# The output product of an attention and MLP kernel: seven block products with fifteen additions in place of eight

## The chip, the cores and the metric

The kernel runs on one core of one Trainium2 chip. The metric is device time in microseconds (us), the median of several runs; the kernel before takes 428.7 us.

Engine names as the profile has them: PE is the matrix engine (TensorE), PEld its weight loads, DVE is VectorE, ACT is ScalarE, POOL is GpSimd, SP is SyncE. A name with q (POOLq, SPq) is that engine's part that issues transfers. Tile names in the views: `st` is a loaded q or k, `c` its cast, `T` its transpose, `pt` the sigmoids, `xT` the attention result as FFN1 reads it, `hT` a block of h, `S` a sum of h, `wT` a sum of weights, `osb` an output tile, `ps_D` a pair of PSUM banks. The ramp is the start, up to about 25 us, in which the first attention tiles are made.

## The reference, cut to what matters

```python
# q, k, v: [8 batches, 12 heads, 448 tokens, 64]; w_gate, w_val: [768, 1536]; w_out: [1536, 768]
scores = q @ k.T / sqrt(64) - log(448)
attn   = sigmoid(scores) @ v                      # [8, 12, 448, 64]
x      = attn.transpose(0, 2, 1, 3).reshape(3584, 768)
h      = silu(x @ w_gate) * (x @ w_val)           # [3584, 1536]   "FFN1"
out    = h @ w_out                                # [3584, 768]    "output product"
```

The change concerns the last line alone. Inputs and output are fp32; the kernel multiplies in fp16 and bf16.

## The kernel before

The eight batches are worked through in four pairs of two. A pair has 24 FFN1 steps (two batches, twelve blocks `f` of 128 hidden features each), then the output product for its 896 tokens, in seven blocks `m` of 128 tokens. Between these units the program places "visits": pieces of attention for batches that come later. Each visit may also cast a q and a k tile that were loaded (`ready`), send them through a transposing DMA, and load the next q, k and v (`fetch`).

```python
def ffn2(pb, m):                      # one 128-token block of the output product: 24 matmuls
    osb = osp.tile([128, DM], FP32, tag="osb", name="osb")        # pool osp has bufs=3
    ...
    for half in range(2):             # output columns 0..383 and 384..767, one PSUM bank each
        for f in range(NF):           # NF = 12
            h = hT[(pb, f)].rearrange("p b s -> p (b s)")         # 128 features x 896 tokens
            nc.tensor.matmul(out=D.t[:, half, :hw], lhsT=h[:, m * 128:(m + 1) * 128],
                             rhs=wo16[f // FW][:, f % FW, half * hw:(half + 1) * hw],
                             start=(f == 0), stop=(f == NF - 1))
    ...                               # two evictions on VectorE into osb, then
    for i in range(2):
        (nc.sync if last else nc.gpsimd).dma_start(out=dsts[i], in_=osb[i * 64:(i + 1) * 64, :])
...
def w_load(kind, i):                  # a quarter of a weight matrix, cast to fp16 on the way
    if kind == "o":
        nc.gpsimd.dma_start(out=wo16[i], in_=moe_w_out[cs, :].rearrange(...))
...
def fetch(n):                         # loads of tile n: all three issued by GpSimd
    load(n, 0, G); load(n, 1, G); load_v(n)
def ready(n):
    cast(n, 0, G); cast(n, 1, G)      # casts on GpSimd
    if n >= NPE:
        trans_dma(n, 0); trans_dma(n, 1)          # issued by SyncE
...
begin[(8, 0)] += [lambda: ready(9), lambda: fetch(11)]            # what a visit starts
...
for i, at in enumerate(((6, 4), (7, 0), (7, 4), (8, 0))):
    begin[at].append(lambda i=i: w_load("o", i))                  # the four quarters of w_out
```

In the traces of this case an engine's instructions and its issues of transfers stand in program order (GpSimd's order after the change, shown below: sums to 104.54, then two casts, then loads, the last `wo` at 108.47). So GpSimd's queue holds the loads of q, k, v and `w_out`, the casts and, for the first three pairs, the output issues, one behind the other.

Of the kernel before, what the change touches and what calls it, by code (L numbers as in the profile page):

```python
# [9 lines left out]
FP32 = mybir.dt.float32  # L10
FP16 = mybir.dt.float16
BF16 = mybir.dt.bfloat16
SIGM = mybir.ActivationFunctionType.Sigmoid
MULT = mybir.AluOpType.mult


@with_exitstack
def kernel(
# [10 lines left out]
    nc = tc.nc  # L29
    ctx.enter_context(tc.manual_schedule())  # L30

    B, H, S, D = q.shape
    DM = H * D
    DFF = moe_w_gate.shape[1]
    C = S // D
    NJ = H // 4
    NP = H // 2
    NF = DFF // 128
# [3 lines left out]
    HREC = 1.0 / HSC  # L42

    qkscale = 1.0 / math.sqrt(D)
    sbias = -math.log(S)

    psD = ctx.enter_context(tc.tile_pool(name="psD", bufs=1, space=bass.MemoryType.PSUM))
    one = ctx.enter_context(tc.tile_pool(name="one", bufs=1))
    stg = ctx.enter_context(tc.tile_pool(name="stg", bufs=9))
    c16 = ctx.enter_context(tc.tile_pool(name="c16", bufs=4))  # L50
    v16p = ctx.enter_context(tc.tile_pool(name="v16p", bufs=6))
    qkT = ctx.enter_context(tc.tile_pool(name="qkT", bufs=4))
    ptp = ctx.enter_context(tc.tile_pool(name="ptp", bufs=10))
    xtp = ctx.enter_context(tc.tile_pool(name="xtp", bufs=12))
    htp = ctx.enter_context(tc.tile_pool(name="htp", bufs=13))
    tmp = ctx.enter_context(tc.tile_pool(name="tmp", bufs=2))
    osp = ctx.enter_context(tc.tile_pool(name="osp", bufs=3))
# [11 lines left out]

    ring = [psD.tile([128, 2, 512], FP32, tag=f"D{i}", name=f"ps_D{i}") for i in range(4)]  # L70
    ring_order = [0, 1, 2, 3]
# [4 lines left out]
    class Banked:  # L76
# [18 lines left out]
        def write(self, ins, bank, uses=None):  # L95
            if bank is not None:
                self.has_mm[bank] = True
                tc.add_to_no_dep_group(self.mm[bank], ins.ins)
                p = self.prev
                if p is not None and p.has_rd[1 - bank] and (uses is None or p.made != uses):  # L100
                    tc.declare_no_dep(ins.ins, group=p.rd[1 - bank], reason="the other bank")
# [9 lines left out]
    FW = 3  # L111
# [3 lines left out]
    wo16 = [one.tile([128, FW, DM], FP16, tag=f"wo{i}", name=f"wo16_{i}") for i in range(NW)]  # L115
# [7 lines left out]
            nc.gpsimd.dma_start(out=dst, in_=w[:, cs].rearrange("(j p) n -> p j n", p=128))  # L123


    qkv_st = {}
    q16, v16, qT = {}, {}, {}

    def src_of(n, which):
        b, j = divmod(n, NJ)  # L130
        return (q, k, v)[which][b, 4 * j:4 * j + 4].rearrange("(h w) (p c) d -> (w p) h (c d)", w=2, c=C)

    def load(n, which, eng=None):
        st = stg.tile([128, 2, S], FP32, tag="stg", name=f"st{which}_{n}")
        (eng or nc.sync).dma_start(out=st, in_=src_of(n, which))  # L135
        qkv_st[(n, which)] = st

# [5 lines left out]
    def cast(n, which, eng, lo=0, hi=C):  # L143
        st = qkv_st[(n, which)]
        if hi == C:
            qkv_st.pop((n, which))
        t = c16.tile([128, hi - lo, 2, D], BF16, tag="c16" if hi - lo == C else f"c16_{lo}", name=f"c16_{which}_{n}")
        q16[(n, which, lo)] = t
        (eng.copy if eng is nc.scalar else eng.tensor_copy)(  # L149
            out=t.rearrange("p c h d -> p h c d"),  # L150
            in_=st.rearrange("p h (c d) -> p h c d", c=C)[:, :, lo:hi, :],
        )
# [96 lines left out]
    hT = {}  # L249
# [13 lines left out]
    def ffn1(b, f):  # L263
        D = Banked("f", made=(b // 2, f))
        for prs in (range(NP - 2), range(NP - 2, NP)) if f == 0 else (range(NP),):
            ffn1_mm(D, b, f, prs)
        ffn1_gate(D, b, f)

    def ffn1_gate(D, b, f):
        s16 = tmp.tile([128, S], FP16, tag="s16", name="s16")  # L270
        D.read(nc.scalar.activation(out=s16, in_=D.t[:, 0, :S], func=SIGM), 0)  # L271
        t1 = tmp.tile([128, S], FP16, tag="t1", name="t1")
        D.read(nc.vector.tensor_tensor(out=t1, in0=D.t[:, 0, :S], in1=s16, op=MULT), 0)  # L273
        if b % 2 == 0:
            hT[(b // 2, f)] = htp.tile([128, 2, S], FP16, tag="hT", name=f"hT_{b // 2}_{f}")
        D.read(
            nc.vector.scalar_tensor_tensor(  # L277
                out=hT[(b // 2, f)][:, b % 2, :], in0=D.t[:, 1, :S], scalar=HSC, in1=t1, op0=MULT, op1=MULT
            ),
            1,  # L280
        )

    def ffn2(pb, m):
        hw = DM // 2
        osb = osp.tile([128, DM], FP32, tag="osb", name="osb")
        dsts = []
        for i in range(2):
            bb, c = divmod(2 * m + i, C)
            bb += 2 * pb
            dsts.append(out[bb * S:(bb + 1) * S, :].rearrange("(p c) n -> c p n", c=C)[c])  # L290
        D = Banked("o")
        for half in range(2):
            for f in range(NF):
                h = hT[(pb, f)].rearrange("p b s -> p (b s)")
                D.write(
                    nc.tensor.matmul(  # L296
                        out=D.t[:, half, :hw],
                        lhsT=h[:, m * 128:(m + 1) * 128],
                        rhs=wo16[f // FW][:, f % FW, half * hw:(half + 1) * hw],
                        start=(f == 0),  # L300
                        stop=(f == NF - 1),
                    ),
                    half,
                    uses=(pb, f),
                )
        last = pb == B // 2 - 1
        end = last and m == C - 1
        for half in range(2):
            hs = slice(half * hw, (half + 1) * hw)
            if end and half == 1:  # L310

                for i in range(2):
                    r = slice(i * 64, i * 64 + 64)
                    oe = osp.tile([128, hw], FP32, tag=f"oe{i}", bufs=1, name=f"oe{i}")
                    if i == 0:
                        ev = nc.scalar.activation(
                            out=oe[r], in_=D.t[r, 1, :hw], func=mybir.ActivationFunctionType.Copy, scale=HREC
                        )
                    else:
                        ev = nc.vector.tensor_scalar(  # L320
                            out=oe[r], in0=D.t[r, 1, :hw], scalar1=HREC, scalar2=None, op0=MULT
                        )
                    D.read(ev, 1)
                    (nc.scalar if i == 0 else nc.sync).dma_start(out=dsts[i][:, hs], in_=oe[r])
            else:
                D.read(
                    nc.vector.tensor_scalar(  # L327
                        out=osb[:, hs], in0=D.t[:, half, :hw], scalar1=HREC, scalar2=None, op0=MULT
                    ),
                    half,  # L330
                )
                if end:
                    for i in range(2):
                        nc.sync.dma_start(out=dsts[i][:, hs], in_=osb[i * 64:(i + 1) * 64, hs])
        if not end:
            for i in range(2):
                (nc.sync if last else nc.gpsimd).dma_start(out=dsts[i], in_=osb[i * 64:(i + 1) * 64, :])  # L337


    FU1, FU2 = 2.26, 3.9  # L340
    units = []
    f1_start, f1_end = {}, {}
    tt = 0.0
    for pb in range(B // 2):
        for b in (2 * pb, 2 * pb + 1):
            f1_start[b] = tt
            for f in range(NF):
                if b or f > 2:
                    units.append((FU1, ffn1, (b, f)))
                tt += FU1  # L350
            f1_end[b] = tt
        for m in range(7):
            units.append((FU2, ffn2, (pb, m)))
            tt += FU2


    FIRST, PER = f1_end[0] - 5.0, 38.5
    tiles = [(n, c) for n in range(NJ, NQ) for c in range(C)]
    visits = [tiles[:2], tiles[2:4]]
    for i in range(0, len(tiles), C):  # L360
# [2 lines left out]
    for grp in visits:  # L363
        n, c = grp[0]
        b, j = divmod(n, NJ)
# [17 lines left out]

    V, G = nc.vector, nc.gpsimd
    load(0, 1, nc.scalar)
    for n, which in ((0, 0), (1, 0), (1, 1), (2, 0), (2, 1), (3, 0), (3, 1)):
        load(n, which)
# [8 lines left out]
    def fetch(n):  # L396
        load(n, 0, G)
        load(n, 1, G)
        load_v(n)

    def ready(n):
        cast(n, 0, G)
        cast(n, 1, G)
        if n >= NPE:
            trans_dma(n, 0)
            trans_dma(n, 1)
# [71 lines left out]
    begin = {(n, c): [] for n in range(NJ, NQ) for c in (0, 4)}  # L478
# [7 lines left out]
    begin[(7, 4)] += [lambda: fetch(10)]  # L486
    begin[(8, 0)] += [lambda: ready(9), lambda: fetch(11)]
    begin[(8, 4)] += [lambda: ready(10)]
    for i, at in enumerate(((6, 4), (7, 0), (7, 4), (8, 0))):
        begin[at].append(lambda i=i: w_load("o", i))  # L490
    for n in range(9, NQ):
# [9 lines left out]
    for dur, fn, args in units:  # L501
        if vi < len(visits) and tcur >= vtime[vi]:
            group = visits[vi]
# [49 lines left out]
```

## Time and profile before

| | before |
|---|---|
| time, median | 428.7 us (428.35 to 429.27, 4 runs) |
| profiled span | 426.6 us |
| PE busy | 415.9 us, 97% |
| output matmuls | 672, 163 ns apart |
| POOL busy | 117.5 us, 28% |
| landing of an output issue | 3.1 us median (GpSimd's queue) |

The views that the prediction reads are shown in it. This is the list of transfers in the stretch 100 to 140 us, around the output product of the first pair: output and source, issuing queue, count, size, median time from issue to landing.

```profile
out_dram<-osb POOLq DMA_DIRECT2D x14, 192.0 KB, 3.2
...
T<-c SPq DMA_TRANSPOSE x8, 5.9
```

Fourteen outputs, seven blocks, land in 3.2 us at the median (7.9 at the longest) although loads and transposes run in the same stretch. A block takes 3.9 us and uses one of three output tiles, and visits come between. So the tile whose output was issued at 108.97 is written again, by VectorE's next eviction into it, only at 120.97, 12 us later.

### The profile page before, as it was taken

What the parts mean: (1) busy time and instruction counts of PE and PEld (TensorE: products, weight loads), DVE (VectorE), ACT (ScalarE), POOL (GpSimd) and SP (SyncE); (2) the same over time, 40 slices, a digit from 0 to 9 for tenths busy, and PEclk for the clock granted to TensorE, in tenths of its full rate; (3) what the DMA queues carried; (4) which work ended last, traced back from release to release, by engine and by line L of the source; (5) the groups of instructions that cost most, each with busy time, mean ns of one, the idle gap of its engine ahead of it and who ended that gap; (6) DMA issues with size and microseconds to landing.
All of it is one profiled execution on the core that took longest, in us unless ns stands there. A gap on an engine that the chain in (4) does not pass through costs nothing.

```text
span 426.6 us, 7903 instructions
## 1 busy us (share of the span) xinstructions
PE 415.9 (97%) x3261; PEld 217.6 (51%) x3261; DVE 204.9 (48%) x337; ACT 211.9 (50%) x291; POOL 117.5 (28%) x167
## 2 busy tenths in 40 slices
PE   6899999999999999999999999999999999999995
PEld 2544544545555444545555544544555545555663
DVE  2726656555324555555323556555433356555322
ACT  4966885654624755656433755746433642222000
POOL 5564346401637346000345545000221100000000
PEclk8799999999999999999999999999999999999999
DMA  8999999995699997500298996600162300000234
GB/s 301 231 277 211 210 190 208 177 247 99 152 218 174 194 174 178 115 0 2 71 229 169 226 193 164 120 0 2 23 131 71 81 0 2 0 2 0 55 94 111
DMA packets 57796, 54.38 MB, mean 127 GB/s; under 512 B 35680, under 2 KB 52448, under 8 KB 57760
## 3 DMA queue, kind: packets, MB, share of 16 engines
q0 software_dynamic: 20896, 39.20, 40.9%
q1 hardware_dynamic: 36512, 14.13, 20.3%
q8 instruction: 25, 0.41, 0.4%
q10 hardware_dynamic: 352, 0.56, 0.4%
q14 instruction: 11, 0.09, 0.1%
HBM read 47.19 MB, written 11.01 MB: 136 GB/s over the span
## 4 chain that ended last, share of the span: by engine, by line
PE 91%; ACT 3%; DVE 2%; issue 1%; DMA 1%; ACTq 0%; DVEq 0%
PE ps_D L256 50%; PE ps_D L296 26%; PE ps_D L197 8%; PE ps_D L228 7%; ACT pt L215 2%; DMA st<-in_q_dram 1%; PE ps_D L171 1%; DVE t L273 1%; ACT s L271 1%; ACT pt L212 1%; DVE T L180 0%; DVE hT L277 0%; DVE xT L237 0%; DVE xT L245 0%; ACT xT L243 0%
## 5 line engine op out<-in xcount | busy, mean ns | idle before, releaser
L215 ACT ACTIVATE pt<-ps_D,sb_t 128x896 f16<-128x896 f32 x148 | 140.3, 1014 | 84.4 <-PE ps_D L197 84.2
L256 PE MATMUL ps_D<-xT,wg 128*128 128x448 f16 x576 | 126.9, 353 | 0.9 <-ACT pt L215 0.5
L256 PE MATMUL ps_D<-xT,wv 128*128 128x448 f16 x576 | 126.4, 352 | 0.0
L296 PE MATMUL ps_D<-wo,hT 128*128 128x384 f16 x672 | 111.8, 326 | 0.0
L273 DVE TENSOR_TENSOR t<-ps_D,s 128x448 f16<-128x448 f32 x96 | 59.9, 624 | 92.3 <-ACT s L271 92.0
L271 ACT ACTIVATE s<-ps_D 128x448 f16<-128x448 f32 x96 | 52.7, 549 | 90.6 <-PE ps_D L256 80.1
L296 PEld LDWEIGHTS <-hT 128*128 128x128 f16 x672 | 64.8, 98 | 46.4 <-issue 4.3
L256 PEld LDWEIGHTS <-wg 128*128 128x128 f16 x576 | 53.7, 98 | 58.5 <-issue 12.4
L256 PEld LDWEIGHTS <-wv 128*128 128x128 f16 x576 | 56.4, 98 | 52.8 <-issue 0.3
L327 DVE TENSOR_SCALAR osb<-ps_D 128x384 f32<-128x384 f32 x55 | 30.7, 558 | 74.2 <-PE ps_D L296 71.0
L277 DVE SCALAR_TENSOR_TENSOR hT<-ps_D,t 128x448 f16<-128x448 f32 x96 | 60.0, 625 | 10.4 <-DVE t L273 0.5
L337 POOL DMA_DIRECT2D out_dram<-osb x42 | 22.4, 537 | 146.1 <-DVE osb L327 146.1
L149 POOL CAST c<-st 128x896 bf16<-128x896 f32 (+1 forms) x42 | 38.8, 936 | 63.1 <-issue 29.6
L197 PE MATMUL ps_D<-T,T 64*64 64x448 bf16 x672 | 47.4, 367 | 2.3 <-ACT T L180 1.1
L228 PE MATMUL ps_D<-pt,v 64*64 64x448 f16 x672 | 36.2, 351 | 0.3 <-ACT pt L215 0.3
L197 PEld LDWEIGHTS <-T 64*64 64x64 bf16 x672 | 16.3, 107 | 25.9 <-issue 18.2
L237 DVE CAST xT<-ps_D 128x448 f16<-128x448 f32 x24 | 15.0, 625 | 29.8 <-PE ps_D L228 23.0
L245 DVE CAST xT<-ps_D 64x448 f16<-64x448 f32 x46 | 28.6, 622 | 0.7
L228 PEld LDWEIGHTS <-v 64*64 64x64 f16 x672 | 19.9, 108 | 13.0 <-issue 1.5
L212 ACT ACTIVATE pt<-ps_D,sb_t 128x448 f16<-128x448 f32 x40 | 23.0, 631 | 0.0
L140 POOL DMA_DIRECT2D v<-in_v_dram x24 | 17.7, 738 | 0.1
L135 POOL DMA_DIRECT2D st<-in_k_dram x20 | 14.7, 736 | 3.1 <-DMA wv<-in_moe_w_val_dram 3.1
(25 smaller groups left out, 59.6 us busy)
## 6 DMA issues: line engine op xcount, KB each, us to landing
st<-in_q_dram POOLq DMA_DIRECT2D x20, 448.0 KB, 4.8
st<-in_k_dram POOLq DMA_DIRECT2D x20, 448.0 KB, 7.0
out_dram<-osb POOLq DMA_DIRECT2D x42, 192.0 KB, 3.1
v<-in_v_dram POOLq DMA_DIRECT2D x24, 224.0 KB, 8.3
wg<-in_moe_w_gate_dram POOLq DMA_DIRECT2D x4, 576.0 KB, 14.4
wv<-in_moe_w_val_dram POOLq DMA_DIRECT2D x4, 576.0 KB, 14.6
wo<-in_moe_w_out_dram POOLq DMA_DIRECT2D x4, 576.0 KB, 14.7
out_dram<-osb SPq DMA_DIRECT2D x12, 192.0 KB, 2.7
```

The source lines that it names most:

```text
L149: (eng.copy if eng is nc.scalar else eng.tensor_copy)(out=t.rearrange("p c h d -> p h c d"), in_=st.rearrange("p h (c d) -> p h c d", c=C) ...
L197: nc.tensor.matmul(out=sc[w * 64:(w + 1) * 64, h2, :S], lhsT=kt[r, w * 64:(w + 1) * 64], rhs=qt[r, :, w * 64:(w + 1) * 64], start=True, st ...
L212: nc.scalar.activation(out=pt[:, h2, :], in_=sc[:, h2, :S], func=SIGM, bias=sb_t, scale=qkscale), h2
L215: nc.scalar.activation(out=pt, in_=sc[:, :, :S], func=SIGM, bias=sb_t, scale=qkscale)
L228: nc.tensor.matmul(out=P[g:g + 64, h2, :S], lhsT=vt[r, h2, c * D:(c + 1) * D], rhs=pt[r, h2, :], start=(c == 0), stop=(c == C - 1),)
L245: nc.vector.tensor_copy(out=o, in_=i)
L256: nc.tensor.matmul(out=D.t[:, i, :S], lhsT=w16[f // FW][:, pr, cs], rhs=xT[(b, pr)], start=(pr == 0), stop=(pr == NP - 1),),
L271: D.read(nc.scalar.activation(out=s16, in_=D.t[:, 0, :S], func=SIGM), 0)
L273: D.read(nc.vector.tensor_tensor(out=t1, in0=D.t[:, 0, :S], in1=s16, op=MULT), 0)
L277: nc.vector.scalar_tensor_tensor(out=hT[(b // 2, f)][:, b % 2, :], in0=D.t[:, 1, :S], scalar=HSC, in1=t1, op0=MULT, op1=MULT),
L296: nc.tensor.matmul(out=D.t[:, half, :hw], lhsT=h[:, m * 128:(m + 1) * 128], rhs=wo16[f // FW][:, f % FW, half * hw:(half + 1) * hw], start ...
L327: nc.vector.tensor_scalar(out=osb[:, hs], in0=D.t[:, half, :hw], scalar1=HREC, scalar2=None, op0=MULT),
```

## The change

The intent is to take matmuls off PE, which is the bound. For two token blocks `g` and `g + 3` of a pair, the 256 tokens by 1536 features of h and the 1536 by 768 of `w_out` are each cut into two by two parts. Eight part products (48 matmuls) become seven (42 matmuls), in Winograd's form of Strassen's algorithm with fifteen additions: four sums of h, four of the weights, seven of products. Part of the seven are made in PSUM, where a product is added onto another; the rest are made by VectorE as it evicts. The sums of h and of the weights go to GpSimd. One block of each pair stays direct, and so does group 0 of the first pair, which is 144 direct matmuls and 11 groups of 42 = 462.

```diff
+    def w_sums():                       # once: 8 instructions of 128 x 1152
+        for s in range(2):
+            ...
+            for kind in (3, 2, 1, 4):
+                ...
+                nc.gpsimd.tensor_tensor(out=t, in0=a, in1=b, op=op)
+    def h_sums(pb, f):                  # per pair: kind 3 for f < 6, the trio 1, 2, 4 for f >= 6
+            ...
+            nc.gpsimd.tensor_tensor(out=t, in0=a, in1=b, op=op)     # 128 x 384
     def ffn1(b, f):
         ...
         ffn1_gate(D, b, f)
+        if b % 2:
+            h_sums(b // 2, f)
+    def ffn2_group(pb, g):              # two blocks, seven products
+        o1 = osp.tile([128, DM], FP32, tag="osb", name="osb")
+        mm(1, 0, True, False)           # product number, PSUM bank, start, stop; 6 matmuls
+        snap(0, o1, 0)                  # evict a bank into a half of an output tile
+        mm(2, 1, True, True)
+        put(1, o1, 0)                   # evict and add onto what the tile holds
+        mm(6, 0, False, False)
+        snap(0, o1, 1)
+        mm(5, 1, True, False)
+        o2 = osp.tile([128, DM], FP32, tag="osb", name="osb")
+        snap(1, o2, 1)
+        mm(7, 0, False, False)
+        put(0, o2, 1)
+        mm(3, 1, False, True)
+        put(1, o1, 1)                   # o1 is complete only here
+        mm(4, 0, False, True)
+        eng = nc.sync
+        ...                             # o1 issued; then snap(0, o2, 0) and o2 issued
@@ schedule @@
-        for m in range(7):
-            units.append((FU2, ffn2, (pb, m)))
+        o_units = [(FU2, ffn2, (pb, C - 1))]
+        for g in range(3):
+            if pb == 0 and g == 0:
+                o_units += [(FU2, ffn2, (pb, m)) for m in (g, g + 3)]
+            else:
+                o_units.append((FU3, ffn2_group, (pb, g)))
-    FIRST, PER = f1_end[0] - 5.0, 38.5
+    FIRST, PER = f1_end[0] - 5.0, 37.3
+    begin[(9, 0)] += [w_sums]
```

Cut: the token and weight slices of the products, the direct blocks, which are now ordered so that the last features come last, smaller pools elsewhere to make room for the sums, and outputs moved from GpSimd's queue to SyncE's. Among the smaller pools are those of the loaded q and k tiles (9 to 4 tiles, the first six apart) and of the v tiles (6 to 5).

## The prediction

> **What bounds the kernel now.** I read the page's busy shares first, then the chain that ended last, then PE's own order of time. Busy shares and chain:
>
> ```profile
> PE 415.9 (97%) x3261; PEld 217.6 (51%) x3261; DVE 204.9 (48%) x337; ACT 211.9 (50%) x291; POOL 117.5 (28%) x167
> ...
> PE 91%; ACT 3%; DVE 2%; issue 1%; DMA 1%; ACTq 0%; DVEq 0%
> ```
>
> PE is busy 97% of the span and is 91% of the chain, so PE's order is the clock of the kernel. A busy PE is not always a PE at its rate, so I took single stretches from the time order of PE, around the end of the first FFN1 pair and in one output block:
>
> ```profile
> 97.83 1.31 PE L256 MATMUL ps_D<-xT,wg 128*128 128x448 f16 x6
> 98.98 1.30 PE L256 MATMUL ps_D<-xT,wv 128*128 128x448 f16 x6
> ...
> 129.72 4.07 PE L296 MATMUL ps_D<-wo,hT 128*128 128x384 f16 x24
> 133.63 0.54 PE L256 MATMUL ps_D<-xT,wg 128*128 128x448 f16 x2
> ```
>
> Columns are start, length, engine. 24 output matmuls take 133.63 - 129.72 = 3.91 us, 163 ns each, with no gap before or after. Removing output matmuls therefore pays in full, if nothing makes PE wait instead. PE has no slack after 22 us in which a new wait could be absorbed.
>
> The other thing to see is GpSimd's order of time, since the change puts work there. Here are the loads of q/k/v (`st`, `v`) and of the output weights `wo` before they are needed:
>
> ```profile
> 60.49 0.72 POOL L135 DMA_DIRECT2D st<-in_q_dram  x1
> 61.21 0.72 POOL L135 DMA_DIRECT2D st<-in_k_dram  x1
> 61.93 0.73 POOL L140 DMA_DIRECT2D v<-in_v_dram  x1
> 62.65 0.78 POOL L120 DMA_DIRECT2D wo<-in_moe_w_out_dram  x1
> ...
> 81.22 0.94 POOL L149 CAST c<-st 128x896 bf16<-128x896 f32 x1 [4.02 <-issue]
> 82.10 0.73 POOL L135 DMA_DIRECT2D st<-in_q_dram  x1
> 82.82 0.74 POOL L135 DMA_DIRECT2D st<-in_k_dram  x1
> 83.54 0.75 POOL L140 DMA_DIRECT2D v<-in_v_dram  x1
> 85.50 0.77 POOL L120 DMA_DIRECT2D wo<-in_moe_w_out_dram  x1 [1.21 <-DMA wo<-in_moe_w_out_dram]
> ```
>
> These issues run well ahead of PE: the first group belongs in the program to an attention visit that PE reaches only at 73.6 us. Even so, in the window 82 to 87 us the last `wo` needs 15.8 us to land, so it is there at 85.5 + 15.8 = 101.3 us. PE starts the output product at 100.1 us and reads the last quarter of `wo` at its tenth matmul, 100.1 + 9 x 0.163 = 101.6 us. The weights arrive **just in time**; the stretches from 60 to 100 us have the DMA share at 0.96 to 1.27, saturated.
>
> **What the Trainium skill says.** "TensorE: Matmul & The Clock Gate", section "Wait — 56ns, not 53.3ns?", gives N/2.4 GHz plus about 2.5 ns per warm matmul: 162.5 ns for N = 384. The trace has 163: it agrees. Its Part 1 says that an idle PE of some 3.4 us drops to half clock and needs about as long to recover; the trace before has no such idle time once started. "GPSIMD Engine Reference", section 3.1, has a two-input `tensor_tensor` at about 2.6 cycles an element, 4497 ns for 2048 fp32; the kernel before has no such instruction, only one-input casts (896 elements, 937 ns). "DMA: Bandwidth & Descriptors", section "SWDGE vs HWDGE vs iDMA", ties a cast during DMA to GpSimd's queue; so the `wo` and `v` loads, which cast to fp16, stay in GpSimd's order, as the trace has them. "SBUF — State Buffer", section "Who interferes with whom", says a VectorE instruction with at most one SBUF input and no 2-port mode does not contend with GpSimd. The gates and evictions here read PSUM plus at most one SBUF tile, and nearly all casts on GpSimd keep to 0.93 to 0.94 us, so I add no contention.
>
> **Part by part.**
>
> *Removed.* The order of the changed program on PE has 144 direct and 462 Strassen output matmuls, 606 for 672: eleven groups save 6 each. 66 x 0.163 = **-10.8 us** on PE, all on the path.
>
> *Added on VectorE.* Seven evictions a group for four: 33 more at 0.558 us (the row `osb<-ps_D`), 18 us on an engine that is 48% busy. Products take 6 x 0.163 = 0.98 us and alternate between two banks, so an eviction (0.56 us and some 0.2 to start) fits behind the other bank's product. Where the xT copies of an attention visit come just ahead (after 129.5 us they hold VectorE to 131.4, when a group begun at 129.7 would want its first eviction at 130.9), the third product waits about 0.4 us. Some four such places: **+1.5 us**.
>
> *Added on GpSimd.* 96 h sums of 384 columns and 8 weight sums of 1152. Estimate from the skill's 4497/2048 = 2.2 ns an element: 0.85 us, with start cost about 0.93 us for an h sum and 2.6 us for a weight sum. A trio that waits on itself is about 3.0 us. In all about 96 x 0.95 + 8 x 2.6 = 112 us, less 42 output issues moved to SyncE (22 us): GpSimd rises from 117 to about 207 us, still under half the span. By share it is harmless; by order it is not.
>
> *Moved: the order on GpSimd.* The first FFN1 pair's h sums stand in GpSimd's order **ahead of** the loads that the visits issue. The order of the changed program reads: sums of f = 0, 1, 2 of the second batch; loads of tile 8 and wo 0; sums 3, 4; casts 8; loads 9, wo 1; sums of 5, 6, 7; loads 10, wo 2; sums of 8, 9, 10; casts 9; loads 11, wo 3. Each sum waits for VectorE's gate of that f, so GpSimd can no longer run ahead of PE. I step through it with PE's times of before:
>
> - gate of f = 2 ends at 74.5 (its `hT` instruction 73.84 + 0.62): sum to 75.6; loads 8 and wo 0, 4 issues, to 78.6; sums 3, 4 to 80.9.
> - casts 8 wait for the k load: issued at 76.4 and landing after 7.2 us (that of 60 to 64 us in the trace before): 83.6, done at 84.8. Loads 9 and wo 1 to 87.8.
> - sum 5 to 88.7, trios 6 and 7 to 94.7; loads 10 and wo 2 to 97.7.
> - trios 8, 9, 10 to 106.7 (gate of 10 done at 96.6: GpSimd is late by its own work); casts 9 to 108.6; loads 11 to 110.8; **wo 3 issued at about 110.8**, not 85.5.
> - The four `wo` loads before landed after 10.1 (little ahead of it) to 19.6 us (two fetches ahead). With 10 to 14: about 121 to 125.
>
> PE needs wo 3 at 101.6 and wo 2 (issued 96.9, there about 108) at 101.1. So the first direct block waits some 20 to 23 us: **+21 us**. A bound that doesn't use my estimate for the sums: the gate of f = 10 at 96.6, three sums of at least 0.5 each, casts 1.8, issues 2.2, landing 10.1 gives 112.2: at least 10.6 us of wait.
>
> *Follow-ups.* An idle PE of this length comes back at half clock, by the skill: **+1.7 us**. The wait then hides the weight sums: they start about 116.5 after the last trio and casts 10 and end by 137.5; PE, resumed at 122.5, has 17 direct matmuls, 48 more, two visits, and two products of group 1 before it reads a weight sum, about 16 us, 138. Later pairs have all loads far ahead; trios of 3.0 us against FFN1 steps of 2.27 put GpSimd about 5 us behind at the end of a pair, which the direct block (3.9 us) and two products cover to within **+0.5 us**.
>
> Sum: 428.7 - 10.8 + 1.5 + 21 + 1.7 + 0.5 = 442.6. I choose 441, a little under, because the skill's rate is for fp32 and fp16 sums may be quicker.
>
> **Rivals.** (1) *The saving arrives whole*: 428.7 - 10.8 + 1 to 3 = 419 to 421. For it: every engine's share allows it, and later pairs show no obstacle. Against it: the lower bound of 10.6 us, which stands on program order and landing times alone. (2) *Quick sums*: at 0.6 us a sum, the same stepping issues wo 3 at 104.7 and lands it at 115: a wait of 13 us and 433. (3) *VectorE takes over*: 33 more evictions, of which two per product pair wait for each other through the banks. At 0.56 of 0.98 us per product I see no bound; if each group lost 0.5 us, 11 x 0.5 = 5.5 us, 446. (4) *The DMA hides it*: if the wo quarter landed in 5 us because queues are empty, 6 us less, 435; the emptiest landing seen is 10.1.
>
> **Range and chances.** 13 us of wait and no extras gives 431; 25 us with all extras 447, with some room for a contention I left out. Range 432 to 449. Within 2% ends at 437.3, that is a wait of about 16 us with the extras: quick sums or a quick landing, 0.14. Faster than 420.1 needs the order argument to be wrong: 0.04.
>
> **What would show it.** In the profile after: (a) PE output matmuls 606, the same 163 ns; (b) one idle stretch of PE near 101 to 122 us, in the first direct block, released by a `wo` DMA; (c) GpSimd's issue of the last `wo` near 110 us, behind h sums; (d) h sums of about 0.9 us, weight sums 2.6; (e) no wait of over 0.6 us within a group on VectorE; (f) later pairs shorter than before by about 2.9 us each. It is wrong if PE shows no idle stretch there (order on GpSimd not binding), if sums take 0.5 us or less, or if a second long wait appears at the weight sums or at the casts behind them.

## The result, and the profile after

The changed kernel is correct and takes **452.05 us** (450.65 to 453.58, 4 runs) against 428.7 us (428.35 to 429.27, 4 runs) of the kernel before in the same rounds. The ratio is 1.0544, 95% interval 1.0502 to 1.0586: slower by 5.4%. A ratio here and below is fast runs compared with fast runs of the same rounds, so it is not quite the ratio of the medians. The profiled run has a span of 451.8 us and a mean granted clock of 0.962. The direction was predicted; the time lies 11 us above the 441 predicted and 3 us above the range.

The busy shares and the chain that ended last, from the page after:

```profile
PE 412.8 (91%) x3195; PEld 212.9 (47%) x3195; DVE 222.7 (49%) x370; ACT 211.8 (47%) x291; POOL 199.7 (44%) x229
...
PE 74%; DMA 9%; POOL 5%; ACT 4%; DVE 4%; issue 2%; SPq 0%; DVEq 0%; ACTq 0%; POOLq 0%
PE ps_D L266 41%; PE ps_D L377 14%; PE ps_D L207 6%; PE ps_D L238 6%; PE ps_D L450 5%; DMA out_dram<-osb 4%; POOL S L340 3%; ACT pt L225 3%; DMA wo<-in_moe_w_out_dram 2%; DMA st<-in_k_dram 1%; POOL st L144 1%; PE ps_D L181 1%; DVE t L285 1%
```

PE has 66 instructions fewer, as intended, and is no longer the chain alone: 9% of the span is waiting for transfers, 5% is GpSimd. The transfer with the largest share is not `wo`, which the prediction spoke of, but an **output**. The time order of PE has both. First the direct blocks behind the first pair's FFN1 (start, length, engine and line, operation, count, then the idle time before it and what ended it):

```profile
101.00 0.98 PE L450 MATMUL ps_D<-wo,hT 128*128 128x384 f16 x5
106.49 0.96 PE L450 MATMUL ps_D<-wo,hT 128*128 128x384 f16 x3 [4.52 <-DMA wo<-in_moe_w_out_dram]
119.18 4.99 PE L450 MATMUL ps_D<-wo,hT 128*128 128x384 f16 x16 [11.72 <-DMA wo<-in_moe_w_out_dram]
124.10 0.76 PE L207 MATMUL ps_D<-T,T 64*64 64x448 bf16 x12
```

A block of 24 matmuls that took 3.9 us before now lasts from 101.00 to 124.10, 23.1 us: 16.24 us of wait for the last two quarters of `wo`, and the last 16 matmuls take 4.92 us, 0.31 each, at about half clock (granted clock 0.54). Here is GpSimd's order of time just ahead of that:

```profile
102.70 0.91 POOL L340 TENSOR_TENSOR S<-S,hT 128x384 f16<-128x384 f16 x1
103.68 0.91 POOL L340 TENSOR_TENSOR S<-hT,S 128x384 f16<-128x384 f16 x1
104.54 1.81 POOL L159 CAST c<-st 128x896 bf16<-128x896 f32 x2
106.29 0.75 POOL L144 DMA_DIRECT2D st<-in_q_dram  x1
107.03 0.73 POOL L144 DMA_DIRECT2D st<-in_k_dram  x1
107.75 0.74 POOL L149 DMA_DIRECT2D v<-in_v_dram  x1
108.47 0.79 POOL L124 DMA_DIRECT2D wo<-in_moe_w_out_dram  x1
```

GpSimd is never idle here; it is late by its own sums, and the last `wo` goes out at 108.47 instead of 85.50. It is there when PE resumes: 119.18 - 108.47 = 10.7 us to landing.

The second loss stands in one group of each of the first two pairs: group 2 of the first pair (from 142.98) and group 1 of the second, the second of its three (from 238.19). PE in the second pair's:

```profile
238.19 2.11 PE L377 MATMUL ps_D<-wo,hT 128*128 128x384 f16 x12
240.15 3.09 PE L377 MATMUL ps_D<-wT,S 128*128 128x384 f16 x18
249.34 2.08 PE L377 MATMUL ps_D<-wo,S 128*128 128x384 f16 x6 [6.11 <-DVE osb L388]
251.21 2.12 PE L377 MATMUL ps_D<-wT,hT 128*128 128x384 f16 x6
```

PE waits for VectorE's eviction at line 388. VectorE, however, is the messenger; its own order of time and the transfers issued in the stretch 237.5 to 240 us say what it waited for:

```profile
248.73 0.56 DVE L388 TENSOR_SCALAR osb<-ps_D 128x384 f32<-128x384 f32 x1 [6.85 <-DMA out_dram<-osb]
```

```profile
out_dram<-osb SPq DMA_DIRECT2D x4, 192.0 KB, 9.8
```

The eviction is the first one into `o2` of group 1. With three tiles and two per group, that is the tile that was `o1` of group 0, the group before; its output was issued from 238.01 on and took 9.8 us to land. In the third pair's groups (337 to 364 us), which also have three tiles and their sums on GpSimd, but no loads beside them, fourteen outputs take 2.9 us at the median and PE's longest wait is 0.24 us. What else was under way shows in GpSimd's order: the q, k and v loads of a visit were issued at 235.28, 236.02 and 236.74, late, behind three trios of sums, and took 4.8, 10.6 and 12.2 us to land; the two transposes issued from 234.49 on took 2.9 and 10.7 us. The table by stretch shows the DMA engines full (busy time of PE, PEld, DVE, ACT and POOL, granted clock, then the mean busy share of the DMA engines, which can exceed 1 in this profile, and GB/s); in the stretch 237 to 240 us before it the share was 0.99:

```profile
240.00:243.00 3.00, 3.00 (x20) 1.83 (x19) 1.12 (x2) 0.00 (x0) 0.93 (x1) 1.00 1.64 144
```

The account of the difference of the spans, 451.8 - 426.6 = 25.2 us, read from these views:

| part | us | how read |
|---|---|---|
| 66 matmuls fewer | -10.8 | 66 x 0.163 |
| direct block, `wo` late | +19.1 | 23.10 - 3.95 (two such blocks take 7.90 before); 16.2 wait, the rest half clock |
| group 2 of pair 1, output tile | +4.7 | 142.98 to 154.57 is 11.6, for 42 x 0.163 = 6.85 |
| group 1 of pair 2, output tile | +8.2 | 238.19 to 253.27 is 15.1, for 6.85 |
| waits for the bank between products | +0.7 | 0.27, 0.23 and 0.24 |
| start | +0.9 | a wait of 0.35 for transposed tiles, and the ramp |
| end | +1.0 | last matmul to end of span: 5.4 for 4.4 |
| not placed | +1.4 | |

Here and below pairs are counted from 1, groups from 0 as in the program.

### The profile page after: what moved, and what is told of

It is laid out like the page before. It is cut to its first block, busy times and chain, and to the rows that moved or that the text cites. A ratio compares the mean times of both kernels' runs of the same rounds, so it can differ in the third digit from the quotient of the medians.

```text
span 451.8 us, 7935 instructions
## 1 busy us (share of the span) xinstructions
PE 412.8 (91%) x3195; PEld 212.9 (47%) x3195; DVE 222.7 (49%) x370; ACT 211.8 (47%) x291; POOL 199.7 (44%) x229
## 4 chain that ended last, share of the span: by engine, by line
PE 74%; DMA 9%; POOL 5%; ACT 4%; DVE 4%; issue 2%; SPq 0%; DVEq 0%; ACTq 0%; POOLq 0%
PE ps_D L266 41%; PE ps_D L377 14%; PE ps_D L207 6%; PE ps_D L238 6%; PE ps_D L450 5%; DMA out_dram<-osb 4%; POOL S L340 3%; ACT pt L225 3%; DMA wo<-in_moe_w_out_dram 2%; DMA st<-in_k_dram 1%; POOL st L144 1%; PE ps_D L181 1%; DVE t L285 1%; DMA st<-in_q_dram 1%; ACT s L283 1%
## 5 line engine op out<-in xcount | busy, mean ns | idle before, releaser
L340 POOL TENSOR_TENSOR S<-hT 128x384 f16<-128x384 f16 x24 | 21.9, 914 | 140.5 <-DVE hT L289 140.5
L450 PE MATMUL ps_D<-wo,hT 128*128 128x384 f16 x144 | 27.1, 348 | 16.2 <-DMA wo<-in_moe_w_out_dram 16.2
L377 PEld LDWEIGHTS <-S 128*128 128x128 f16 x264 | 26.1, 99 | 28.4 <-issue 12.1
L388 DVE TENSOR_SCALAR osb<-ps_D 128x384 f32<-128x384 f32 x43 | 24.0, 557 | 31.1 <-PE ps_D L377 19.2
L377 PE MATMUL ps_D<-wT,S 128*128 128x384 f16 x198 | 34.0, 326 | 0.7 <-DVE osb L388 0.7
L207 PEld LDWEIGHTS <-T 64*64 64x64 bf16 x672 | 16.2, 107 | 27.3 <-issue 19.0
L450 PEld LDWEIGHTS <-hT 128*128 128x128 f16 x144 | 14.6, 103 | 28.4 <-issue 20.5
L377 PEld LDWEIGHTS <-hT 128*128 128x128 f16 x198 | 19.5, 101 | 15.5 <-issue 4.2
## 6 DMA issues: line engine op xcount, KB each, us to landing
v<-in_v_dram POOLq DMA_DIRECT2D x24, 224.0 KB, 10.1
```

The source lines that it names most:

```text
L207: nc.tensor.matmul(out=sc[w * 64:(w + 1) * 64, h2, :S], lhsT=kt[r, w * 64:(w + 1) * 64], rhs=qt[r, :, w * 64:(w + 1) * 64], start=True, st ...
L340: nc.gpsimd.tensor_tensor(out=t, in0=a, in1=b, op=op)
L377: nc.tensor.matmul(out=D.t[:, bank, :hw], lhsT=l, rhs=B_(i), start=(first and i == 0), stop=(i == HF - 1), skip_group_check=True,),
```

## The experiments

Every run is correct. Each is given by its edit to the changed kernel, unless it says otherwise. **Theory**, as it stood before e10 (at first I took the queue of the outputs for the second exit): all of the loss comes from GpSimd's order, by two exits: the output weights are issued late, and a visit's loads are issued late so that outputs share the DMA engines with them and an output tile comes free late. **Rivals:** the queue that issues the outputs is at fault; three tiles are too few for the groups whatever GpSimd does; the seven products themselves cost more on PE or VectorE than they save.

### The late output weights: e1_wo_early

```diff
-    for i, at in enumerate(((6, 4), (7, 0), (7, 4), (8, 0))):
+    for i, at in enumerate(((5, 4), (5, 4), (6, 0), (6, 0))):
         begin[at].append(lambda i=i: w_load("o", i))
```

> The four loads of the output weights are put ahead of the h sums in GpSimd's order (at the visits (5,4) and (6,0) instead of (6,4) to (8,0)); nothing else changes. My theory (they were late because they stood behind h sums that wait for gates): the two waits of PE for them in the first direct block (4.5 + 11.7 us) and the half clock after them vanish, about 19 us. PE then reaches the weight sums earlier, which end near 129 us on GpSimd while PE wants them near 118 to 121: a new wait of some 8 us in group 1. Net about 452 - 19 + 8 = 441. Rival A (DMA bandwidth is the limit up to 100 us, not the order): loads of q, k and v become late instead, PE waits at attention visits, time stays near 450. Rival B (weight sums need no wait): about 433.

Measured: 447.37 us (446.1 to 448.08), ratio 1.0413 (1.0389 to 1.0436). The `wo` waits are gone, so program order was their cause. But the gain is some 5 us, where 19 less 8 were expected, because PE reaches the groups earlier and now meets GpSimd at the next thing it owes. The PE time order of this run:

```profile
126.44 2.08 PE L377 MATMUL ps_D<-wT,S 128*128 128x384 f16 x6 [6.52 <-POOL wT L320]
...
144.27 2.08 PE L377 MATMUL ps_D<-wo,S 128*128 128x384 f16 x6 [5.79 <-DVE osb L388]
```

6.5 us are waited for the weight sums, which the long `wo` wait had hidden, and the first output-tile wait grows from 2.83 to 5.79 us. The second is 4.29 us for 6.11, and 1.45 us are waited for transposed tiles. A wait taken away was mostly turned into others.

### No sums used, all products direct: e4_sums_direct

```diff
-            if pb == 0 and g == 0:
+            if True:
                 o_units += [(FU2, ffn2, (pb, m)) for m in (g, g + 3)]
```

> All output blocks are computed directly (672 output matmuls as before the change), but all h sums and weight sums are still made on GpSimd and not used. Theory (the sums' place in GpSimd's order makes the output weights late, whatever the products are): the same two waits in the first direct block, 16 us, with half clock 19; no wait for output tiles, since a block uses one tile each 3.9 us. 428.7 + 19 to 20 = 448. Rival (the waits come from the Strassen products or from VectorE's extra evictions): 430.

Measured: 452.13 us median, fast runs 451.04 to 453.2, ratio 1.0518 (1.0485 to 1.0552). All sums are still computed, nobody reads them, and PE has its 672 matmuls back. The waits for `wo` are the same two, 5.22 and 11.42 us; there is no wait for an output tile. So the sums cost some 22 us without a single product that uses them, and with direct blocks the output tiles are no problem. (The other edits, the smaller pools above all, are in this run too; e7 and e10 below have them as well and are not slower than the kernel before.) It is 4 us over the 448 expected; 1.04 us of that is a wait for `xT`, the rest I did not place. The equality with the changed kernel is a coincidence of two sums: here 10.8 us are not saved, there 12.9 us are lost on output tiles.

### The queue of the outputs: e3_out_act and e3b_out_pool

```diff
-        eng = nc.sync
+        eng = nc.scalar                           # e3_out_act
+        eng = nc.sync if last else nc.gpsimd      # e3b_out_pool
```

> The outputs of the Strassen groups are issued on ScalarE's DMA queue instead of SyncE's; nothing else changes. Theory (the outputs lie in SyncE's queue behind the DMA transposes, land after 7 to 10 us, and the three output tiles don't come free in time): outputs land in about 3 us, the waits of VectorE for output tiles (3.6, 6.9, 1.4 us) and the half clock after two of them vanish, 452 - 12 = 440. Rival (the 16 DMA engines themselves are full of transposes, whichever queue issues): landing stays at 7 to 10 us near 142 and 238 us, time stays above 449.

> The outputs of the Strassen groups of the first three pairs are issued by GpSimd again, as all outputs were before the change; direct blocks keep SyncE. Theory (transposes ahead in SyncE's queue): outputs land in 3 to 5 us, waits for output tiles vanish, about 440, the same as on ScalarE's queue. Rival (DMA engines full): no gain. A second rival: GpSimd, now waiting for evictions, delays casts and loads of later tiles, and PE waits at attention visits.

Measured: 461.18 us (458.91 to 463.63), ratio 1.0757 (1.0715 to 1.0798), for ScalarE's queue; 449.67 us (448.37 to 451.49), ratio 1.0473 (1.0439 to 1.0506), for GpSimd's. Both miss the 440 expected. I had taken SyncE's queue, which also carries the transposes, for the cause. It is not: in the second pair's groups (205 to 245 us) the outputs land no sooner from either queue. ScalarE's in the first fence, GpSimd's in the second:

```profile
out_dram<-osb ACTq DMA_DIRECT2D x4, 192.0 KB, 9.0
```

```profile
out_dram<-osb POOLq DMA_DIRECT2D x4, 192.0 KB, 9.4
```

This is what the Trainium skill says in "DMA: Bandwidth & Descriptors", section "Issuing engines are not separate DMA queues": transfers started by any engine end up on the same 16 DMA engines and interleave there. The runs agree for this stretch: 9.8, 9.0 and 9.4 us from three queues. I had read past it. In the first pair's group GpSimd's queue did help (3.4 us, the wait gone); the loads of that visit then stand behind the outputs in the same order, which delays them, but I have not shown that this is why. ScalarE's queue costs 9 us in addition. Half of that is seen: its issues wait for evictions and stand before its sigmoids, and PE waits of 1.90, 1.22 and 1.42 us for `pt` at visits appear. The rest is not placed.

### A fourth output tile: e2_osb4

```diff
-    v16p = ctx.enter_context(tc.tile_pool(name="v16p", bufs=5))
+    v16p = ctx.enter_context(tc.tile_pool(name="v16p", bufs=4))
-    htp = ctx.enter_context(tc.tile_pool(name="htp", bufs=13))
+    htp = ctx.enter_context(tc.tile_pool(name="htp", bufs=12))
-    osp = ctx.enter_context(tc.tile_pool(name="osp", bufs=3))
+    osp = ctx.enter_context(tc.tile_pool(name="osp", bufs=4))
```

> The changed kernel with four output tiles instead of three (room from one spare h tile and one v tile); nothing else. Theory (an output takes 7 to 10 us to land while transposes and loads fill the DMA engines, and with three tiles a group rewrites the first output of the group before it about 5 us after its last eviction): the waits of PE through VectorE for output tiles (2.8 and 6.1 us) and the half clock after them (about 2 us each) vanish: 452 - 12 = 440. Rival (VectorE is late for another reason, and the DMA is only named by the profile): above 449. Second rival: the spare v tile was needed, loads of v wait and PE waits at attention visits: 445 or more.

Measured: 443.61 us (441.56 to 444.51), ratio 1.0313 (1.0269 to 1.0358). Of the two waits, 2.83 and 6.11 us, only 0.83 us in the second pair is left. The gain, 1.0544 - 1.0313 = 0.0231 of 429 us, is 10 us, somewhat less than the 12.9 of the account; that sum held the half clock after the waits, and in other runs of this kernel than the profiled one (441.56, the fastest) I cannot see where the rest went. The outputs that the changed kernel waited for still land late (those of the first pair's group 1 in 5.5 us at the median, of the second pair's group 0 in 9.6); the tile is no longer waited for.

### Both: e5_wo_osb, and then the weight sums on VectorE: e6_wo_osb_wdve

e5 is e1 and e2 together. e6 is e5 with the eight weight sums moved to VectorE, one behind each gate from f = 4 on of the first pair's second batch:

```diff
         ffn1_gate(D, b, f)
+        if b == 1 and f >= 4:
+            if not w_step:
+                w_step.append(w_sums())           # now a generator
+            next(w_step[0])
...
-                nc.gpsimd.tensor_tensor(out=t, in0=a, in1=b, op=op)
+                yield nc.vector.tensor_tensor(out=t, in0=a, in1=b, op=op)
...
-    begin[(9, 0)] += [w_sums]
```

> Early output weights and four output tiles together. The two causes are separate in time, so the gains should add: 447 - 12 = 435, with one long wait left, 6.5 us for the weight sums in group 1 and its half clock. Rival (one of the two hides the other): above 439.

> As the last, and the eight weight sums move from GpSimd (2.37 us each in one block of 19 us) to VectorE, one behind each gate of f = 4 to 11 of the second batch. If the weight sums' place on GpSimd is the last of the long waits, what remains is the saving of 10.8 us less about 3 us of small waits: 421 to 423. A weight sum on VectorE is expected at 0.7 to 1.4 us, 6 to 11 us in all beside PE. Rival (VectorE and GpSimd block each other when both read two tiles: VectorE's gates become late): 426 or more.

Measured: e5 432.62 us (431.87 to 434.33), ratio 1.0070 (1.0030 to 1.0110); e6 427.12 us (426.13 to 428.04), ratio 0.9936 (0.9901 to 0.9972). Neither cure hides the other: e5 takes 20 us off the changed kernel, more than the 5 and 10 us of the two alone. (In e1 the output-tile waits were 10.1 us together, for 8.9 in the changed kernel; the rest of the surplus is not placed.) What is left in e5 is the wait for the weight sums, 6.32 us, 1.69 us for transposed tiles and 0.98 us for an output tile. e6 removes the first and is 4 us over what I expected, in the range of its rival. Its PE time order has a single wait over 0.4 us after the ramp:

```profile
117.10 0.96 PE L207 MATMUL ps_D<-T,T 64*64 64x448 bf16 x8 [3.02 <-DMA T<-c]
```

It is a transposed tile whose cast stands in GpSimd's order behind the h sums, the third thing that this order delays. After it PE runs at half clock for some 6 us (granted clock 0.50 to 0.51 from 117.1 to 123): the eight matmuls take 0.96 us, 0.57 elsewhere. Some sums became slower too, as the rival had it. The two weight sums of the kind `wT<-wo,wo` take 0.98 us on VectorE in the mean, for 0.75 with no sums on GpSimd (run e7 below), and single h sums on GpSimd that overlap them take 1.3 us for 0.91 (VectorE's order of time, then GpSimd's, of e6):

```profile
98.37 1.19 DVE L324 TENSOR_TENSOR wT<-wo 128x1152 f16<-128x1152 f16 x1
```

```profile
98.04 0.91 POOL L346 TENSOR_TENSOR S<-S,hT 128x384 f16<-128x384 f16 x1
99.03 1.30 POOL L346 TENSOR_TENSOR S<-hT,S 128x384 f16<-128x384 f16 x1
```

The Trainium skill has this in the section that the prediction quotes for the opposite case ("SBUF — State Buffer", "Who interferes with whom"): a VectorE instruction with two SBUF inputs contends with a GpSimd instruction that reads SBUF. The trace agrees in part: the weight sum and the second h sum shown, which overlap, take 1.19 and 1.30 us, while the h sum before, which overlaps too but was under way when the weight sum began, has its usual 0.91. How much of e6's 4 us this is, no run shows. The evictions, which have PSUM and at most one SBUF input, do not show it: 557 ns after, 558 before.

### All sums on VectorE: e7_sums_dve

The `wo` loads stand where the changed kernel has them, and there are four output tiles as in e2.

```diff
-                nc.gpsimd.tensor_tensor(out=t, in0=a, in1=b, op=op)    # weight sums
+                nc.vector.tensor_tensor(out=t, in0=a, in1=b, op=op)
-            nc.gpsimd.tensor_tensor(out=t, in0=a, in1=b, op=op)        # h sums
+            nc.vector.tensor_tensor(out=t, in0=a, in1=b, op=op)
-    begin[(9, 0)] += [w_sums]
+    begin[(8, 4)] += [w_sums]
```

> All sums, of h and of the weights, on VectorE, four output tiles, the output weights loaded where the change loads them. My theory says that the order on GpSimd is what made them late: without sums there GpSimd runs ahead again as before the change, the wait for output weights is gone although their loads haven't moved. An h sum on VectorE about 0.3 us, a trio near 1 us with its waits: VectorE nearly as full as PE in second batches, so 421 to 426. Rival (the late output weights have to do with the DMA, not with the order): the wait of 16 us is still there, 440.

Measured: 429.51 us (427.78 to 430.16), ratio 0.9982 (0.9937 to 1.0027). With the sums gone from GpSimd the last `wo` is waited for 0.72 us although its place in the program is the one that cost 16 us. This supports the theory's first half, but GpSimd is only 9 us earlier than in the changed kernel, not 23 as before the change: it waits here for something else, a free tile for v (GpSimd's order of time; this run has 4 tiles of v, the changed kernel 5, the kernel before 6):

```profile
98.38 0.72 POOL L149 DMA_DIRECT2D v<-in_v_dram  x1 [12.03 <-PE ps_D L238]
99.10 0.78 POOL L124 DMA_DIRECT2D wo<-in_moe_w_out_dram  x1
```

The last `wo` is there in time because it also lands in 5.9 us, for 10.7, and because PE comes 1.9 us later to its block. So e1, which moves the loads alone, is the cleaner test. In the changed kernel GpSimd's order shows no wait for a free tile before the last `wo`. The sums are shorter here (groups by shape: count, busy us, mean ns; e7's first, then two of the changed kernel):

```profile
L340 DVE TENSOR_TENSOR S<-hT,hT 128x384 f16<-128x384 f16 x24 | 10.8, 451 | 0.8
...
L320 DVE TENSOR_TENSOR wT<-wo,wo 128x1152 f16<-128x1152 f16 x2 | 1.5, 748 | 0.0
```

```profile
L340 POOL TENSOR_TENSOR S<-hT,hT 128x384 f16<-128x384 f16 x24 | 22.0, 918 | 5.9 <-DVE hT L289 5.9
...
L320 POOL TENSOR_TENSOR wT<-wo,wo 128x1152 f16<-128x1152 f16 x2 | 4.7, 2364 | 0.0
```

But VectorE is now busy 264.2 us (62%) and late at visits: PE waits 1.41 and 2.27 us for VectorE's copies `xT`, and 0.4 to 0.5 us at three other places. The whole saving goes there and into some 5 us that I could not place. My 421 to 426 was a miss.

### Whose fault are three tiles: e10_dve_osb3

e7 with one edit, and therefore without GpSimd's lateness:

```diff
-    osp = ctx.enter_context(tc.tile_pool(name="osp", bufs=4))
+    osp = ctx.enter_context(tc.tile_pool(name="osp", bufs=3))
```

> As e7_sums_dve (all sums on VectorE, so that GpSimd is not behind), with three output tiles again as in the changed kernel. Theory (the output tiles come free late because GpSimd, behind with its sums, sends the loads and casts of a visit off just before or during a Strassen group, so that the outputs share the DMA engines with them): no lateness, so outputs still land in about 3 us as in e7, the waits for an output tile stay under 1 us in all, and the time is that of e7, 429 to 431. Rival (the second tile of a group comes too early after the first tile's output in any case, three tiles are too few for the order of evictions): waits of about 3 and 6 us return, 436 to 441.

Measured: 429.51 us (428.92 to 431.39), ratio 1.0019 (0.9991 to 1.0047), the time of e7. One wait for an output tile is left, of 0.70 us, and the outputs of the first pair's groups (115 to 145 us) land as in a quiet stretch (PE time order, then transfers):

```profile
225.90 1.14 PE L377 MATMUL ps_D<-wo,S 128*128 128x384 f16 x6 [0.70 <-DVE osb L388]
```

```profile
out_dram<-osb SPq DMA_DIRECT2D x12, 192.0 KB, 2.8
```

So three tiles suffice, but for 0.7 us, when GpSimd is not behind with sums. The shift is small: in the second pair the visit's q load goes out 4.7 us before group 1 begins, for 2.9 us in the changed kernel, and its transposes 7.1 us before, for 3.7; group 0's outputs land in 4.2 to 4.7 us, for 9.8. No run moves the loads and the transposes apart, so which of the two fills the DMA engines more is not shown. The output-tile wait is the second exit of the same cause: late sums, therefore late loads and transposes, therefore full DMA engines just when a tile has to come free.

### Sharing the sums: e8_split, e9_split_g0 and e11_split_osb3

e8 is e6 with the h sums shared between the two engines, and with the last group's second half sent off earlier; e9 also computes the first group by seven products; e11 is e9 with three output tiles.

```diff
-            nc.gpsimd.tensor_tensor(out=t, in0=a, in1=b, op=op)
+            (nc.vector if kind in (1, 3) else nc.gpsimd).tensor_tensor(out=t, in0=a, in1=b, op=op)
...
         put(0, o2, 1)
+        if end:                                   # sent after put(0, o2, 1), not after the last product
+            for i in range(2):
+                nc.sync.dma_start(out=out_rows(pb, g + 3)[i][:, hw:], in_=o2[i * 64:(i + 1) * 64, hw:])
... e9 also:
-            if pb == 0 and g == 0:
-                o_units += [(FU2, ffn2, (pb, m)) for m in (g, g + 3)]
-            else:
-                o_units.append((FU3, ffn2_group, (pb, g)))
+            o_units.append((FU3, ffn2_group, (pb, g)))
```

> As e6_wo_osb_wdve, with the h sums split: kinds 1 and 3 on VectorE at 0.36 to 0.45 us each instead of 0.9 us on GpSimd, kinds 2 and 4 stay on GpSimd, and the last group sends the second output half of its other tile off right after its eviction. Theory (what is left over in e6 is the wait of the transposes of tile 9 behind the sums on GpSimd, 3.0 us, the half clock after it, about 1.5, and the tail, 1.0): 427.1 - 3.0 - 1.5 - 1.0, so 420 to 422, with no TensorE wait over 1 us around 117 us. Rival (VectorE and GpSimd now hold each other up through the tiles of the sums, or VectorE comes late as with all sums on it): waits of 0.5 to 2 us on VectorE in the groups, 424 to 428.

> As e8_split, and the first group of the first pair is computed by the seven products too instead of direct (504 matmuls of products and 96 direct, 600 in place of 606). Theory: 6 matmuls fewer are 0.98 us, so 419 to 421. Rival: the first group then needs its weight sums and h sums some 6 us earlier, while GpSimd is still behind, and TensorE waits 2 to 4 us there: 422 to 425.

> As e9_split_g0, with three output tiles in place of four. In e9 the outputs of the groups land in 4.7 us at the median, against 7.1 and 9.8 in the changed kernel. Theory: waits of 0 to 1.5 us in the groups of pairs 1 and 2, 422 to 425. Rival as above: 430 or more.

Measured: e8 423.05 us (422.92 to 423.82), ratio 0.9859 (0.9842 to 0.9875); e9 **422.04 us** (421.88 to 422.44), ratio 0.9831 (0.9817 to 0.9846), both against 429.52 us (428.8 to 429.77) in five rounds; e11 426.49 us (423.49 to 426.54), ratio 0.9911 (0.9873 to 0.9950). e9 is the fastest version, 1.7% faster than the kernel before; that is clear of noise. e6, e8 and e11 also lie below the kernel before. Its PE waits around the first groups, from its time order:

```profile
99.30 0.57 PE L207 MATMUL ps_D<-T,T 64*64 64x448 bf16 x8 [1.47 <-DVE hT L293]
102.70 4.06 PE L457 MATMUL ps_D<-wo,hT 128*128 128x384 f16 x24 [0.45 <-DVE xT L255]
118.92 3.08 PE L383 MATMUL ps_D<-wT,S 128*128 128x384 f16 x18 [0.24 <-DVE osb L394]
```

The saving of 72 x 0.163 = 11.7 us would have given a span of 426.6 - 11.7 = 414.9; it is 420.1. (About 1 us of the difference lies in the kernel before itself, which took 429.5 us in these rounds and 428.4 in its profiled run.) Of the 5.2 us 3.7 are waits that can be listed, the longest the 1.47 us behind VectorE's weight sums. Both e8 and e9 came out 1 us over their theory's ranges; e9 lies at the low end of its rival's. e11, with half of the h sums still on GpSimd, has output-tile waits of 1.45 and 2.84 us, more than my theory's 1.5 and less than the rival's; they lie between the changed kernel's 8.94 us in all (all sums on GpSimd) and e10's 0.70 (none), which is the order that the cause asks for. One of e11's four runs took 423.5 us and three 426.5, so its size is less certain.

## Why the prediction was right or wrong

**Right: the cause and the direction.** PE is the bound, its saving is -10.8 us, and GpSimd's order takes more than that away. The output matmuls are 606 (point a). PE's idle stretch is at 101.98 to 119.18, released by `wo` (b), in two pieces, since the quarter before the last was late too. The last `wo` is issued at 108.47, for about 110.8 predicted (c), and lands after 10.7 us, at the short end of the 10 to 14 assumed; both make the term too large. An h sum takes 0.91 us for 0.93 estimated, a weight sum 2.36 for 2.6 (d). Rival 2 falls on these, rival 1 on the wait itself, rival 3 on VectorE's 0.7 us, rival 4 on the 10.7 us of landing. e1 confirms the mechanism: with the loads ahead of the sums in that order, nothing waits for `wo`. The lower bound of 10.6 us was none, though: it took 10.1 us as the least landing, and in e7 and e10 the last `wo` landed in 5.9 and 6.2 us.

**Right in kind, a little large: "+21" and "+1.7".** Together 22.7 us predicted, 19.1 measured. This surplus hid part of what was missed below; that was luck.

**Wrong: the step "Follow-ups", where later pairs were put "to within +0.5 us".** Measured: 12.9 us, 4.7 in group 2 of the first pair and 8.2 in group 1 of the second. The step had GpSimd about 5 us behind at the end of a pair, which it was, but asked only whether the sums and the loads come in time for PE. It did not ask what the late loads, issued behind the sums, collide with. They and the late transposes filled the DMA engines while the outputs went out, and the time from issue to landing of an output went from about 3 us to 7.4 and 9.8.

**Wrong for the same reason: "Added on VectorE".** It lets an eviction wait for its bank alone and prices this at +1.5 us (measured 0.7, three short waits). An eviction also waits for the tile it writes. Before the change that tile had 12 us to land. A group now holds two of three output tiles, and `o2` of the next group takes over the tile of `o1` when that group's fourth product is done, 4 to 5 us after `o1` was issued (issued at 238.01, the product done about 242.1). Any longer landing is waited for. Point (e), no wait of over 0.6 us within a group, fails with 3.57 and 6.85 us on VectorE. e2 (a fourth tile) and e10 (no lateness) each remove the wait, by different ends.

**Point (f), later pairs 2.9 us shorter each,** fails for the second pair. For the third and fourth together, the end of one pair's output product to the end of the last is 185.3 us for 187.7 before, 2.4 us less and not 5.8. Most of that is no loss: 36 output matmuls fewer in this stretch (5.9 us) stand against 44 attention matmuls more (2.2 us, as one visit of 44 takes in PE's order), which the changed visit times moved into it, and 0.6 us of short waits; 0.7 us is not placed.

**The sum again with the measured terms:** 428.7 - 10.8 + 0.7 + 19.1 + 12.9 + 1.9 for start and end = 452.5, for 452.05 measured. The terms are those of the profiled run, which took 453.58 us, so the agreement looks better than the account is: that leaves 1.4 us unplaced. The range was wrong because every rival varied a term that was in the sum; none asked for a resource that the sum did not name.

## What to carry to other kernels

Work that is put on a half idle engine is not free if that engine also issues transfers in program order: look at what stands behind it in the order, first at the loads, then at what the late loads will share the DMA engines with. For every instruction that is added, list each thing it waits for, the buffer that it writes too, and compare the time until that buffer is written again with the longest landing seen, not the median. When a wait is cured, expect PE to meet the same late engine at its next debt (`wo`, then weight sums, then transposed tiles), and cure the lateness as well as the waits: here the cures of two waits (e5) brought +5.4% to +0.7%, and only moving part of the sums to VectorE too (e9, which also computes one more group by seven products) brought it to -1.7%.

## What the Trainium skill lacked or had wrong

- "GPSIMD Engine Reference", section 3.1, has one size in fp32 only for the two-input sum (4497 ns for 2048). The runs show fp16: 0.91 us for 384 and 2.36 us for 1152 elements a partition, so (2364 - 914) / 768 = 1.9 ns an element and about 0.2 us fixed, where the page's figure gives 2.2 ns. An estimate from the page was 2 to 10% too long. The same section's fp32 ratio of the two engines (1.96) does not carry over: VectorE takes 0.36 to 0.45 us for 384 and 0.75 for 1152, which is 2.0 to 2.5 and 3.1 times as fast as GpSimd.
- "SBUF — State Buffer", section "Who interferes with whom", states that VectorE and GpSimd contend when VectorE reads two SBUF inputs, which the runs confirm in part (above), and gives no size for this case. With sums on both, single ones took 1.2 us for 0.75 on VectorE and 1.3 for 0.91 on GpSimd.
- "DMA: Bandwidth & Descriptors" was right on the queues and lacks a landing time under mixed load. A write of 192 KB landed in 2.9 us in a quiet stretch and in 7.4 to 9.8 us beside three loads of 1.1 MB in all and two transposes.
- "TensorE: Matmul & The Clock Gate", Part 1, gives about 3.4 us as the idle time that leads to half clock. The runs show it after less, and not each time: 2.83 us of wait in the changed kernel was followed by six matmuls in 1.71 us (half clock), 2.84 us in e11 by six in 0.97 us (full clock).
